# Half-size products for four of eight feature pairs, two banks for the second product, and a listed order of steps

## The chip, the core and the metric

The kernel runs on one core of one Trainium2 chip. The metric is the device time of one execution in microseconds (us). Before the change it is 716.3 us, the median of three executions (715.98 to 716.58).

## The reference

An attention across channels is followed by a two-layer network with a tanh GELU. All inputs and the output are float32.

```python
# q, k, v: (4, 6080, 256); w_in: (256, 2048); w_out: (2048, 256)
qn = q / (norm(q, axis=1) + 1e-6);  kn = k / (norm(k, axis=1) + 1e-6)
s = kn.transpose(0, 2, 1) @ qn / tau            # (4, 256, 256)
a = softmax(s, axis=-1)
x = (v @ a).reshape(24320, 256)
h = x @ w_in                                    # (24320, 2048)
g = 0.5 * h * (1 + tanh(c * (h + 0.044715 * h**3)))
out = g @ w_out                                 # (24320, 256)
```

## The kernel before, in words

For each of the four batches the kernel forms the Gram matrix of q and k (256 x 256) and the column norms, and from them the attention matrix. That matrix is multiplied into `w_in` once per batch (`aw_part`, L422), which leaves one 256 x 2048 matrix `AW`. So h = v @ AW, and the tokens see two matrix products: the first (256 to 2048 features) and, after the GELU, the second (2048 to 256).

**Blocks.** Tokens are taken in blocks of 512, twelve in a batch (the last has 448), 48 in all, numbered n. In the loop at the end of the kernel each block has eight stages, one per pair p of feature chunks (two chunks of 128 features, so 256 features a pair).

**First product.** `mm1` (L442, matmuls at L450) does a pair with four matmuls of 512 columns (two feature chunks, two halves of the 256 input channels), into a pair of banks of PSUM, the memory that TensorE writes to. There are two such pairs of banks (pool `pH`). One ScalarE instruction (L454) applies the GELU to both chunks, 1024 elements a partition, and writes bf16 to `g`.

**Second product.** It runs one block behind. It is already a 2 x 2 Strassen-Winograd product: the features in two halves, the tokens of a block in two halves, seven products instead of eight. Each product (`product`, L531, matmuls at L546) is eight matmuls of 256 columns. Its left factors, sums of parts of `w_out`, are made once. Its right factors are sums of parts of `g`, made per block on VectorE (DVE): t1 at L517 (2048 elements), t2, t3, t4 at L528 to L530 (1024 elements, two calls each). The seven products accumulate in three single banks (`r`, `p`, `q` of pool `pM`): ScalarE copies partial results out (`keep`, L555), DVE adds them to later ones (`add_out`, L562) and transposes the outcome in 32 x 32 squares (`turn`, L570), and four DMAs store it (`store`, L647).

**The next batch, meanwhile.** In blocks 1 to 7 of a batch the rows of q and k of the next one, loaded as bf16 through GpSimd's queue (`load_one`, L93), go through the Gram product, two matmuls of 256 columns per 128 rows (`gram_row`, L213). ScalarE squares q (L165), DVE squares k (L166), and DVE folds the squares into one 128 x 512 float32 tile (`sum_rows`, L188 to L202). In block 8 DVE splits that tile into three bf16 parts (`split`, L242 to L246) whose columns TensorE sums with twelve one-column matmuls (`ss_cols`, L259). Blocks 9 to 11 form the scores, the row sums and `AW` of the next batch.

**Order.** Everything is issued in the order of the program text (`manual_schedule`); every engine runs its own instructions strictly in that order, and the framework adds the waits. The loop calls, in each stage p, `mm1` with its GELU, then one product of the second product, then what that stage has of sums, Gram row, fold and chain.

The kernel's pool `pM` has four tags of one bank each: `a` (Gram, then products into `AW`), `q`, `p`, `r`.

Of the kernel before, what the change touches and what calls it, by code (L numbers as in the profile page):

```python
# [17 lines left out]
def kernel(  # L18
# [38 lines left out]
    tsp = ctx.enter_context(tc.tile_pool(name="tsp", bufs=2))  # L57
# [6 lines left out]

    pM = ctx.enter_context(tc.tile_pool(name="pM", bufs=1, space=bass.MemoryType.PSUM))
    pH = ctx.enter_context(tc.tile_pool(name="pH", bufs=2, space=bass.MemoryType.PSUM))


    def chunks_of(b):
        sizes = [8, 7, 8, 8, 8, 6, 2] if b == 0 else [7, 7, 7, 7, 7, 7, 5]  # L70
        assert sum(sizes) == R
        res, r0 = [], 0
        for n in sizes:
            res.append((r0, n))
            r0 += n
        return res
# [77 lines left out]

    def squares(b, c):
        qt, kt = qk_tiles[b, c]
        r0, n = chunks_of(b)[c]
        rest = with_rest(b, c)
        sq = sqp.tile([128, 8, 512], BF16, tag="sq")
        if rest:  # L160
            nc.vector.memset(sq[REM:, n, :], 0.0)
        if n <= 2:
            nc.vector.tensor_mul(sq[:, 0:n, 0:256], qt[:, 0:n, :], qt[:, 0:n, :])
        else:
            nc.scalar.activation(sq[:, 0:n, 0:256], qt[:, 0:n, :], AF.Square)  # L165
        nc.vector.tensor_mul(sq[:, 0:n, 256:512], kt[:, 0:n, :], kt[:, 0:n, :])  # L166
        if rest:
            nc.scalar.activation(sq[:REM, n, 0:256], qt[:REM, n, :], AF.Square)
            nc.vector.tensor_mul(sq[:REM, n, 256:512], kt[:REM, n, :], kt[:REM, n, :])
        SQ[b, c] = sq  # L170
# [11 lines left out]
    def sum_rows(b, c):  # L182

        sq = SQ.pop((b, c))
        n = len(rows_of(b, c))
        assert n in (6, 7)
        a1 = addp.tile([128, 4, 512], BF16, tag="a1")
        nc.vector.tensor_add(a1[:, 0:3, :], sq[:, 0:3, :], sq[:, 3:6, :])  # L188
        a2 = addp.tile([128, 2, 512], FP32, tag="a2")
        nc.vector.tensor_add(a2[:, 0, :], a1[:, 0, :], a1[:, 1, :])  # L190
        if n == 7:
            nc.vector.tensor_add(a2[:, 1, :], a1[:, 2, :], sq[:, 6, :])
        rest = a2[:, 1, :] if n == 7 else a1[:, 2, :]
        if b not in ACC:
            acc = accp.tile([128, 512], FP32, tag="acc")
            ACC[b] = acc
            nc.vector.tensor_add(acc, a2[:, 0, :], rest)
        else:
            acc = ACC[b]
            a3 = addp.tile([128, 512], FP32, tag="a3")  # L200
            nc.vector.tensor_add(a3, a2[:, 0, :], rest)
            nc.vector.tensor_add(acc, acc, a3)  # L202

    def gram_row(b, c, i):
        if (b, c, i) == (b, 0, 0):
            G[b] = pM.tile([128, 2, 256], FP32, tag="a", name=f"G{b}")
# [3 lines left out]
        first = c == 0 and i == 0  # L210
        last = c == len(chunks_of(b)) - 1 and i == len(rows) - 1
        for jc in range(2):
# [4 lines left out]
                start=first and jc == 0, stop=last and jc == 1)  # L217

    def ss_rows(c, which):
# [3 lines left out]
        if c == 0:  # L223
            SS[which] = pM.tile([128, 2] if which == 0 else [128, 256], FP32,
                                tag="qp"[which], name=f"ss0{which}")
# [14 lines left out]
    def split(parts, rest, x):  # L240

        nc.vector.tensor_copy(parts[0], x)  # L242
        nc.vector.tensor_sub(rest, x, parts[0])
        nc.vector.tensor_copy(parts[1], rest)
        nc.vector.tensor_sub(rest, rest, parts[1])
        nc.vector.tensor_copy(parts[2], rest)  # L246

    def ss_split(b):
        parts = addp.tile([128, 4, 512], BF16, tag="a1", name=f"parts{b}")
        rest = addp.tile([128, 2, 512], FP32, tag="a2", name=f"rest{b}")  # L250
        split([parts[:, i, :] for i in range(3)], rest[:, 0, :], ACC[b])
        ACC[b] = parts

    def ss_cols(b):

        SS[b] = pM.tile([128, 4], FP32, tag="q", name=f"ss{b}")
        for j in range(4):
            for i in range(3):
                nc.tensor.matmul(SS[b][:, j : j + 1], lhsT=ACC[b][:, i, j * 128 : j * 128 + 128],  # L259
                                 rhs=ones_bf[:, 0:1], start=j == 0 and i == 0,  # L260
                                 stop=j == 3 and i == 2)
# [46 lines left out]
    def first_aw():  # L308
# [3 lines left out]
        ps = [pM.tile([128, 512], FP32, tag="qp"[ic], name=f"aw_ps{ic}") for ic in range(2)]  # L312
# [37 lines left out]
    def k_factors(b):  # L350
# [6 lines left out]
        parts = smx.tile([128, 3, 2], BF16, tag="parts")  # L357
        rest = smx.tile([128, 2], FP32, tag="rest")
        split([parts[:, i, :] for i in range(3)], rest, rr[:, 2:4])
        NRM[b] = (parts, rh)  # L360

    def k_row(b):

        parts, rh = NRM[b]
        dg = smx.tile([128, 3, 2, 128], BF16, tag="dg")
        for i in range(3):
            for ic in range(2):
                nc.vector.tensor_mul(dg[:, i, ic, :], ident_bf,
                                     parts[:, i, ic : ic + 1].to_broadcast([128, 128]))
# [91 lines left out]

# [353 lines left out]
```

## Time and profile before

| what | value |
|---|---|
| time, median of 3 | 716.3 us |
| granted TensorE clock | 0.999 of full speed |
| TensorE (PE) busy | 693.9 us, 4885 matmuls |
| VectorE (DVE) busy | 521.5 us, 950 instructions |
| ScalarE (ACT) busy | 485.9 us, 590 instructions |
| first product, L450, 512 columns | 1344 + 64 matmuls (and 128 of 448 columns) |
| second product, L546, 256 columns | 2464 matmuls (and 224 of 224 columns) |
| Gram rows, L213 | 368 matmuls of 256 columns |
| GELU, L454, 1024 elements | 352 instructions, 1024 ns each |
| t2, t3, t4, 1024 elements | 88 each, 0.67 to 0.68 us each |

The profile gives for each engine the time in which at least one of its instructions ran. Matmuls overlap in the pipeline, so a matmul's duration (about 0.38 us for 512 columns) is longer than the slot it takes in the stream; the distance from one start to the next gives the slot. The chain of waits follows the work that ended last back to its start. A timeline row merges equal instructions: start, length, engine, line, operation, count.

### The profile page before, as it was taken

The page shows a single profiled execution, that of the slowest core. Times are in us where ns is not written, and L with a number is a line of the kernel's source. Part 1 is how long each engine was busy: PE and PEld are TensorE (multiplying, and loading weights), DVE is VectorE, ACT ScalarE, POOL GpSimd, SP SyncE. Part 2 cuts the span into 40 slices and gives each one's busy share as a digit, 9 for nine tenths or more (in the row PEclk, how much of TensorE's full clock was granted, in tenths as well). Part 3 has the DMA queues.
Part 4 walks back from the last instruction along what each step waited for, and adds up shares of the span by engine and source line. Part 5 has one row for each costly group of instructions (what it writes and reads, how often), then busy time and mean ns, then how long its engine had stood idle before and what let it go on. Part 6 is the DMA issues. An engine that isn't in the chain of part 4 may idle for free.

```text
span 716.3 us, 12307 instructions
## 1 busy us (share of the span) xinstructions
PE 693.9 (97%) x4885; PEld 467.7 (65%) x4885; DVE 521.5 (73%) x950; ACT 485.9 (68%) x590; POOL 67.1 (9%) x125
## 2 busy tenths in 40 slices
PE   3899999999999999999999999999999999999997
PEld 2756666666666666666666666666666666666665
DVE  4589878778957887878875778788786465564565
ACT  5387667766677677666767676676677666666673
POOL 4320011100001011101001010110000000000000
PEclk9999999999999999999999999999999999999999
DMA  9998778832558888744427787775334336354122
GB/s 241 208 253 149 135 124 143 132 64 58 98 84 132 141 145 131 128 80 94 80 59 140 99 153 132 126 125 102 58 72 99 62 68 103 67 95 81 43 59 56
DMA packets 161402, 79.19 MB, mean 111 GB/s; under 512 B 150368, under 2 KB 153184, under 8 KB 160352
## 3 DMA queue, kind: packets, MB, share of 16 engines
q0 software_dynamic: 12576, 39.46, 34.9%
q1 hardware_dynamic: 147664, 37.67, 25.3%
q10 hardware_dynamic: 1104, 1.28, 0.6%
q8 instruction: 38, 0.62, 0.4%
q14 instruction: 20, 0.16, 0.1%
HBM read 78.91 MB, written 36.83 MB: 162 GB/s over the span
## 4 chain that ended last, share of the span: by engine, by line
PE 90%; DMA 5%; DVE 2%; issue 1%; ACT 0%; POOL 0%; DVEq 0%; POOLq 0%
PE hp L450 44%; PE r L546 23%; PE p L546 11%; PE q L546 5%; PE G L213 5%; DMA t<-in_k_dram 4%; PE ps L426 2%; DMA t<-in_q_dram 1%; DVE sq L166 0%; DVE c L562 0%; DVE ot L570 0%; PE ss L237 0%; DVE t L530 0%; DVE a L177 0%; DVE wcomb L499 0%
## 5 line engine op out<-in xcount | busy, mean ns | idle before, releaser
L454 ACT ACTIVATE g<-hp 128x1024 bf16<-128x1024 f32 (+1 forms) x384 | 386.7, 1015 | 195.8 <-PE hp L450 191.4
L450 PE MATMUL hp<-vT,aw 128*128 128x512 bf16 (+1 forms) x1472 | 370.2, 377 | 0.0
L546 PEld LDWEIGHTS <-wcomb 128*128 128x128 bf16 x2688 | 262.5, 98 | 101.6 <-issue 6.1
L450 PEld LDWEIGHTS <-aw 128*128 128x128 bf16 x1536 | 149.5, 98 | 110.1 <-issue 1.1
L546 PE MATMUL r<-t,wcomb 128*128 128x256 bf16 (+1 forms) x1152 | 148.1, 271 | 1.4 <-DVE c L562 1.1
L562 DVE TENSOR_TENSOR c<-r,y 128x256 f32<-128x256 f32 (+1 forms) x95 | 39.9, 420 | 50.5 <-PE r L546 42.9
L213 PE MATMUL G<-t 128*128 128x256 bf16 (+1 forms) x368 | 64.3, 273 | 3.3 <-DMA t<-in_k_dram 3.3
L530 DVE TENSOR_TENSOR t<-t,g 128x1024 bf16<-128x1024 bf16 (+1 forms) x96 | 65.0, 677 | 0.0
L529 DVE TENSOR_TENSOR t<-g 128x1024 bf16<-128x1024 bf16 (+1 forms) x96 | 64.9, 676 | 0.0
L562 DVE TENSOR_TENSOR c<-q,x 128x256 f32<-128x256 f32 (+1 forms) x48 | 20.1, 419 | 60.9 <-PE q L546 56.6
L528 DVE TENSOR_TENSOR t<-g,t 128x1024 bf16<-128x1024 bf16 (+1 forms) x96 | 63.3, 659 | 0.4
L570 DVE STREAM_TRANSPOSE ot<-c 128x256 f32<-128x256 f32 (+1 forms) x144 | 57.6, 425 | 1.9 <-DVE c L562 0.2
L132 POOL DMA_DIRECT2D vb<-in_v_dram x46 | 23.6, 512 | 376.8 <-PE hp L450 376.8
L517 DVE TENSOR_TENSOR t<-g 128x2048 bf16<-128x2048 bf16 (+1 forms) x48 | 57.7, 1203 | 0.0
L165 ACT ACTIVATE sq<-t 128x1792 bf16<-128x1792 bf16 (+3 forms) x26 | 43.1, 1657 | 9.8 <-DMA t<-in_q_dram 9.8
L546 PE MATMUL q<-g,wcomb 128*128 128x256 bf16 (+1 forms) x384 | 49.3, 271 | 0.0
L546 PE MATMUL p<-t,wcomb 128*128 128x256 bf16 (+1 forms) x384 | 49.3, 271 | 0.0
L546 PE MATMUL p<-g,wcomb 128*128 128x256 bf16 (+1 forms) x384 | 49.3, 271 | 0.0
L546 PE MATMUL r<-g,wcomb 128*128 128x256 bf16 (+1 forms) x384 | 49.3, 271 | 0.0
L213 PEld LDWEIGHTS <-t 128*128 128x128 bf16 (+1 forms) x368 | 35.6, 98 | 12.5 <-issue 4.6
L570 DVE STREAM_TRANSPOSE ot<-r 128x256 f32<-128x256 f32 (+1 forms) x48 | 21.4, 445 | 30.6 <-PE r L546 30.6
L166 DVE TENSOR_TENSOR sq<-t 128x1792 bf16<-128x1792 bf16 (+4 forms) x27 | 28.1, 1042 | 11.7 <-DMA t<-in_k_dram 11.4
(110 smaller groups left out, 344.3 us busy)
## 6 DMA issues: line engine op xcount, KB each, us to landing
out_dram<-ot SPq DMA_DIRECT2D x176, 128.0 KB, 2.4
vb<-in_v_dram POOLq DMA_DIRECT2D x42, 256.0 KB, 4.7
t<-in_q_dram POOLq DMA_DIRECT2D x19, 448.0 KB, 5.2
t<-in_k_dram POOLq DMA_DIRECT2D x19, 448.0 KB, 4.9
wst<-in_moe_w_out_dram POOLq DMA_DIRECT2D x2, 1024.0 KB, 10.2
t<-in_q_dram POOLq DMA_DIRECT2D x3, 512.0 KB, 15.0
t<-in_k_dram POOLq DMA_DIRECT2D x3, 512.0 KB, 16.9
out_dram<-ot SPq DMA_DIRECT2D x12, 112.0 KB, 4.9
```

Source lines behind the costliest of these rows:

```text
L165: nc.scalar.activation(sq[:, 0:n, 0:256], qt[:, 0:n, :], AF.Square)
L166: nc.vector.tensor_mul(sq[:, 0:n, 256:512], kt[:, 0:n, :], kt[:, 0:n, :])
L213: nc.tensor.matmul(G[b][:, jc, :], lhsT=qt[:np_, r, jc * 128 : jc * 128 + 128], rhs=kt[:np_, r, :], start=first and jc == 0, stop=last and ...
L450: mm = nc.tensor.matmul(hp[:, u, :cols], lhsT=AW[b][:, cc, fc * 128 : fc * 128 + 128], rhs=vt_tiles[n][:, cc, :cols], start=cc == 0, stop= ...
L454: nc.scalar.activation(GS[n][:, 2 * p : 2 * p + 2, :cols], hp[:, :, :cols], AF.Gelu_apprx_tanh)
L517: nc.vector.tensor_sub(t1[:, :, :hc], quarter(n, 0, 1), quarter(n, 0, 0))
L528: nc.vector.tensor_sub(v[2], b22, v[1])
L529: nc.vector.tensor_sub(v[3], b22, quarter(n, 0, 1, f0, f1))
L530: nc.vector.tensor_sub(v[4], v[2], quarter(n, 1, 0, f0, f1))
L546: nc.tensor.matmul(ACCS[n, acc][:, :hc], lhsT=wcomb[:, w, fc, :], rhs=x, start=first and fc == 0, stop=fc == 7, skip_group_check=True)
L562: nc.vector.tensor_add(CS[n][:, tj, ci, :hc], ACCS[n, acc][:, :hc], XS[n, name][:, :hc])
L570: nc.vector.transpose(OT[n][:, tj * nb : tj * nb + nb, ci, :], src.rearrange("p (x t) -> p x t", t=32))
```

## The change

**Half-size products in the first product (`small`, `set_step`, `sums_w`, `sums_v`).** Two pairs of feature chunks form a set; the sets are pairs (1, 2) and (5, 6). A set is a 2 x 2 product: feature pair by half of the input channels, times half of the input channels by half of the tokens. In place of 2 pairs x 4 matmuls of 512 columns it does seven products m1 to m7, two matmuls of 256 columns each. The left factors are parts of `AW` and four sums of them (`sums_w`, eight DVE operations a batch); the right factors are parts of v and four differences (`sums_v`, three DVE operations a block). A set uses one pair of banks `qp` and one single bank `rb` (tag `s`). Its steps, for set i, by their names in the lists:

- `m1` into rb; `cq`: ScalarE copies rb to the first half of qp, where `m2` will be added; `m5` into the second half of qp; `y5`: ScalarE copies that to SBUF (`yw`).
- `m6` is added to rb; `ap`: DVE writes rb + yw to the second half of qp, where `m3` will be added.
- `m7` is added to rb; `ax`: DVE writes rb + yw to SBUF (`xw`); `m4` is added to rb.
- GELUs: `Gq` from qp (1024 elements), `Gr` from rb (512), `Gx` from xw (512).

Blocks 0 and 1 and blocks 10 and 11 of batches 0 to 2 have no set and block 2 has one; all others have two.

**Second product in two banks.** It now uses `r` and `p` only (in blocks without sets `s` also, for one product). The fifth product stays in `p` after being copied; DVE writes r + copy back to `p` (`ap`), where the third product is added; `p` is then transposed straight from PSUM. A product is issued in two halves (`M1A`, `M1B`), the sums in halves (`T2a`, `T2b`, ...).

**A listed order.** A block's steps follow one of three lists, GRAM, PLAIN and NO_SETS. A name ending in -1 means that step for the block before, -2 two before, +1 one ahead; g0 is the first product of pair 0, G0 its GELU, w0m1 step m1 of set 0, M1A the first half of product 1, c11 to c22 and c11a the second product's adds and transposes, e0 to e7 the places for loads and for the chain to the next batch. Where the list changes from one block to the next, steps that the new one has with a shorter lag are issued first.

**The Gram stage.** Eight chunks of six rows (the last five and a rest) in blocks 1 to 8 in place of seven; both squares on ScalarE; the fold in single steps f1 to f5. The splits into three bf16 parts go: the column sums take four one-column float32 matmuls and the row of k factors one float32 matmul of 256 columns. ScalarE copies the Gram matrix to SBUF, and the chain to the next batch moves to blocks 9 to 11.

The core of the diff:

```diff
-    tsp = ctx.enter_context(tc.tile_pool(name="tsp", bufs=2))
+    tsp = ctx.enter_context(tc.tile_pool(name="tsp", bufs=1))
+    t4p = ctx.enter_context(tc.tile_pool(name="t4p", bufs=2))
...
-    pH = ctx.enter_context(tc.tile_pool(name="pH", bufs=2, space=bass.MemoryType.PSUM))
+    pH = ctx.enter_context(tc.tile_pool(name="pH", bufs=1, space=bass.MemoryType.PSUM))
...
-        sizes = [8, 7, 8, 8, 8, 6, 2] if b == 0 else [7, 7, 7, 7, 7, 7, 5]
+        sizes = [8, 7, 8, 8, 8, 6, 2] if b == 0 else [6, 6, 6, 6, 6, 6, 6, 5]
...
-            for i in range(3):
-                nc.tensor.matmul(SS[b][:, j : j + 1], lhsT=ACC[b][:, i, j * 128 : j * 128 + 128],
-                                 rhs=ones_bf[:, 0:1], start=j == 0 and i == 0,
-                                 stop=j == 3 and i == 2)
+            nc.tensor.matmul(SS[b][:, j : j + 1], lhsT=ACC[b][:, j * 128 : j * 128 + 128],
+                             rhs=ones_f[:, 0:1], start=True, stop=True)
...
-        for i in range(3):
-            nc.tensor.matmul(ps, lhsT=ones_bf, rhs=dg[:, i], start=i == 0, stop=i == 2)
+        nc.tensor.matmul(ps, lhsT=ones_f, rhs=dg, start=True, stop=True)
...
+    def small(n, i, m):
...
+        lhs, rhs = {1: (aw(pa, 0), v[:, 0, lo]), 2: (aw(pa, 1), v[:, 1, lo]),
+                    3: (sw(4), v[:, 1, hi]), 4: (aw(pb, 1), tv[:, 3, :hc]),
+                    5: (sw(1), tv[:, 0, :hc]), 6: (sw(2), tv[:, 2, :hc]),
+                    7: (sw(3), tv[:, 1, :hc])}[m]
+        if m == 1:
+            RB[n, i] = pM.tile([128, 512], FP32, tag="s", name=f"rb{n}_{i}")
+        dst = {2: 0, 3: 1, 5: 1}
+        acc = qp(n, i)[:, dst[m]] if m in dst else RB[n, i]
...
+        for u in range(2):
+            nc.tensor.matmul(acc[:, u * hc : u * hc + hc], lhsT=lhs[:, u * 128 : u * 128 + 128],
+                             rhs=rhs, start=m in (1, 5) and u == 0, stop=u == 1,
+                             skip_group_check=True)
...
+    def set_step(n, i, what):
...
+        if what == "cq":
+            nc.scalar.activation(qp(n, i)[:, 0, :c], RB[n, i][:, :c], AF.Copy)
+        if what == "y5":
+            YW[n, i] = xp.tile([128, 512], FP32, tag="yw", name=f"yw{n}_{i}")
+            nc.scalar.activation(YW[n, i][:, :c], qp(n, i)[:, 1, :c], AF.Copy)
+        if what == "ap":
+            nc.vector.tensor_add(qp(n, i)[:, 1, :c], RB[n, i][:, :c], YW[n, i][:, :c])
+        if what == "ax":
+            XW[n, i] = xp.tile([128, 512], FP32, tag="xw", name=f"xw{n}_{i}")
+            nc.vector.tensor_add(XW[n, i][:, :c], RB[n, i][:, :c], YW.pop((n, i))[:, :c])
...
+    GRAM = steps(
+        "g0 c21-2 w1Gr-1 e0 c11-3 w0m5 G0 row3 T2a-1 M1A-1 w0m1 T2b-1 M1B-1 w0cq c11a-2 g3 "
+        "e1 w0y5 T3b-1 cq-1 w0m6 row1 G3 w0ap M5A-1 M5B-1 e2 T3a-1 qsq w0m7 M6A-1 w0ax row5 "
+        "M6B-1 c22-2 y5-1 w0m4 T4b-1 e3 w0m3 w0Gr w0m2 w1m5 ap-1 row0 w0Gq f3-1 row2 w1m1 "
+        "M3A-1 vs+1 e4 w1cq M3B-1 w1y5 row4 T4a-1 w1m6 g4 w0Gx w1ap e5 M7A-1 c12-1 G4 w1m7 "
+        "T1a w1m3 w1m2 M7B-1 ksq M2A-1 w1ax e6 g7 ax-1 w1Gx f1 M4B-1 w1Gq w1m4 e7 M4A-1 "
+        "f4-1 M2B-1 G7 f2")
+    PLAIN = steps(
+        "g0 c11a-2 w1Gr-1 c22-2 e0 M1A-1 G0 T3b-1 w0m1 w0m5 M1B-1 T2b-1 w0cq M5A-1 e1 T2a-1 "
+        "w0y5 w0m6 M5B-1 w0ap g3 y5-1 T4b-1 cq-1 e2 w0m7 G3 M6A-1 w0ax M6B-1 w0m3 e3 ap-1 "
+        "w0m4 w1m5 T3a-1 w0Gr w0m2 M3A-1 w0Gq M3B-1 w1m1 e4 c12-1 M7A-1 w1cq vs+1 g4 w0Gx "
+        "w1y5 T4a-1 w1m6 e5 M7B-1 G4 w1ap M2A-1 M2B-1 ax-1 w1m2 c11-2 e6 w1m3 w1m7 w1Gq "
+        "M4A-1 w1ax g7 T1a w1Gx e7 M4B-1 G7 w1m4 c21-1")
...
+            if (blk, p) == (9, 2):
+                for k in range(1, 6):
+                    todo((f"f{k}", n - 1))
...
+        CHAIN = {
+            (9, 0): [g_copy],
+            (9, 3): [ss_cols, norms],
+            (9, 5): [k_factors, k_row],
+            (9, 7): [k_row_pe],
+            (10, 0): [scores_b, lambda b: scores_c(b, 0)],
...
+            (11, 0): [row_sums],
+        }
```

## The prediction

> **What bounds the kernel now.** I read the page's busy times first, then the stages, then single instructions. Busy share by engine, and the chain of waits:
>
> ```profile
> PE 693.9 (97%) x4885; PEld 467.7 (65%) x4885; DVE 521.5 (73%) x950; ACT 485.9 (68%) x590; POOL 67.1 (9%) x125
> ...
> PE 90%; DMA 5%; DVE 2%; issue 1%; ACT 0%; POOL 0%; DVEq 0%; POOLq 0%
> ```
>
> TensorE (PE) is busy for 97% and carries 90% of the chain; the rest is mostly the loading at the start. A busy share is only an average, so I asked for busy times over single blocks (columns: length; busy time and count of PE, weight loads, DVE, ACT, POOL; clock; DMA share; GB/s): a block with Gram rows, the one after it, one of the last batch.
>
> ```profile
> 294.90:309.40 14.50, 14.48 (x103) 9.75 (x101) 11.75 (x21) 10.26 (x12) 2.65 (x5) 1.00 0.76 123
> ...
> 323.90:337.00 13.10, 13.10 (x100) 8.81 (x99) 10.07 (x27) 8.71 (x12) 1.53 (x2) 1.00 0.37 70
> ...
> 573.00:586.00 13.00, 13.00 (x89) 8.61 (x88) 7.54 (x15) 8.93 (x11) 0.49 (x1) 1.00 0.47 83
> ```
>
> TensorE never pauses in any of them. So the time is the sum of matmul slots, and nothing but fewer slots (or new pauses) moves it. The slot comes from starts, not durations, since matmuls overlap. Timeline of one block:
>
> ```profile
> 326.53 1.03 PE L450 MATMUL hp<-vT,aw 128*128 128x512 bf16 x4
> ...
> 327.40 1.04 PE L546 MATMUL q<-g,wcomb 128*128 128x256 bf16 x8
> ...
> 328.27 1.03 PE L450 MATMUL hp<-vT,aw 128*128 128x512 bf16 x4
> ```
>
> Four 512-column matmuls take 0.87 us, eight 256-column ones 0.87: 0.2175 and 0.109 us each, exactly by columns. A plain block is 32 x 0.2175 + 56 x 0.109 = 13.0 us; 14 Gram matmuls add 1.5, as the windows show.
>
> The other engines must be priced by spacing too. DVE back to back:
>
> ```profile
> 324.32 0.69 DVE L528 TENSOR_TENSOR t<-g,t 128x1024 bf16<-128x1024 bf16 x1
> ...
> 324.93 0.69 DVE L529 TENSOR_TENSOR t<-g 128x1024 bf16<-128x1024 bf16 x1
> ...
> 325.53 0.68 DVE L530 TENSOR_TENSOR t<-t,g 128x1024 bf16<-128x1024 bf16 x1
> ```
>
> A sum of 0.68 to 0.69 us costs 0.60 in a full queue: 0.08 overlaps. And two group rows for prices:
>
> ```profile
> L454 ACT ACTIVATE g<-hp 128x1024 bf16<-128x1024 f32 x352 | 357.8, 1024 | 183.6 <-PE hp L450 179.8 <-DVE aw L433 1.8
> ...
> L562 DVE TENSOR_TENSOR c<-q,x 128x256 f32<-128x256 f32 x44 | 18.6, 423 | 53.5 <-PE q L546 49.2 <-ACT g L454 4.3
> ```
>
> [...] the trace has 1024 ns for 1024 elements [...] and two gelus in 1.94 us from 323.26, so 0.92 apart. [...] the trace has 692 ns at 512 and 423 from PSUM at 256, [...] no fp32 matmul is in this trace.
>
> **The change, part by part.**
>
> *Half-size products.* Listed by block: n=0, 1 and the six blocks 10 and 11 of batches 0 to 2 have no set, n=2 has one, the other 39 two: 79 sets. A set replaces 8 matmuls of 512 columns (1.74 us) by 14 of 256 (1.526): 0.217 saved. 77 x 0.217 + 2 x 0.19 (last block, 448 columns) = **-17.1 us**. There are six more weight loads per set, at 98 ns each below the 109 ns slot, so they stay under the matmuls as L546's do.
>
> *What the sets put elsewhere.* Per set ACT gets two 512-element copies (the first product, PSUM to PSUM; the fifth, to SBUF) and three gelus (1024, 512, 512) for two of 1024. Unseen forms; by the 256-element keep (385 ns) and the 1024-element gelu a 512 one is 0.60 us, spaced 0.50. DVE gets two 512-element fp32 adds (0.69, spaced 0.61); per block 0.98 us of token differences. A plain block with two sets then needs, in spacings, ACT 4 x 0.92 + 2 x (0.92 + 4 x 0.50) + 2 x 0.27 = 10.1 us, and DVE 12.0 us by durations (0.98 + 4 x 0.69 + 1.21 + 6 x 0.68 + 7 x 0.43), 10.5 by spacings, against 12.57 on TensorE. A Gram block (12 Gram matmuls now) is 13.88 on TensorE; both squares on ACT make 10.1 + 2 x 1.37 = 12.8; the fold on DVE (0.91 + 3 x 0.69) makes 15.0 by durations, but 25 x 0.08 overlaps: 13.0. So each engine is left some per cent, DVE least.
>
> *Whether the order fits.* I walked the lists, each PE step at its slot, releases 0.2 us after a slot's end (hp started 301.39, slot to 302.26, gelu at 302.45). Plain block, times from its start: w0m1 ends 1.52, but ACT has the previous set's last gelu until 0.95 and G0 at 1.07 to 1.98, so w0cq runs 1.98 to 2.58; w0m6 is due at 2.60. y5 ends 3.07; DVE does c21, c11a, c22, T3b, T2b, T2a until 3.1, then w0ap to 3.8; w0m7 is due at 4.12. w0ax 4.54 to 5.23, w0m4 due 5.42. Second set: cq ends 7.96 (due 8.46), ap 9.7 (10.41), ax 11.5 (12.37). Banks: w1m5 at 5.64 needs G3's end 5.34; c21 is out at 0.5, the first second-product at 0.87. Behind a late w0cq would stand y5, G3 and the rest of ACT; behind a late w0ap all DVE sums, for which the second product waits. Gram block: w0ap ends 4.36 (due 4.55), w0ax 5.68 (5.85), w1m6's copy 8.27 (8.46), w1ap 9.6 (9.98); DVE's fold waits for the k squares at 12.1 and ends 0.4 into the next block, where c21 is needed only at 1.30. Slack is 0.02 to 0.5 us everywhere, nothing is late. I take 0.05 us lost per block with sets, **+2 us** (0 to 0.25, so 0 to 10).
>
> *Loads.* The k load is issued behind g4's matmuls (9.5 in the block), and row3 uses it 5.4 us later, where it had 7:
>
> ```profile
> t<-in_k_dram POOLq DMA_DIRECT2D x19, 448.0 KB, 4.9
> ...
> t<-in_k_dram POOLq DMA_DIRECT2D x3, 320.0 KB, 4.2
> ```
>
> 384 KB between these: 4.55 us plus 0.2, so 0.6 spare. Free.
>
> *The chain to the next batch.* Out of PE go 36 one-column matmuls (0.30 us per 12 by starts), 9 of 256 columns (1.0 us) and 12 one-column row sums (0.4): -2.3. In come 12 one-column fp32 and three 256-column fp32 matmuls; [...]: +2.9. Net **+0.5** (-1.5 to +4). In block 9 two folds (0.69 each) are queued ahead of w0ax, which then ends at 6.4 where w0m4 is due at 5.42, and the column sums wait for them: 1.0 us, three times, **+3** (0 to 6). DVE's five-op splits that go relieve a queue that did not bind.
>
> *Second product in two banks, steps in a list.* Same 56 matmuls, same keeps less one (ACT 0.27 us), an add and turns as before: no PE slot changes. Costed at nothing, TensorE's stream being the cover. At the twelve switches between lists leftover steps are flushed at once ahead of the new list: 0.1 each, **+1.2**. At the end one more set's gelu stands before the last sums: **+0.5**.
>
> Sum: 716.3 - 17.1 + 2 + 0.5 + 3 + 1.2 + 0.5 = 706.4, say **706.5 us**.
>
> **Rivals.** *All of it is kept* (no pauses; matmul slots alone): 716.3 - 17.1 + 0.5 and the tail's 0.5 give 700. For it: my walk found no late step in a steady block. Against: block 9. *DVE becomes the bound in Gram blocks*: if it does not overlap, 15.0 against 13.88 us over 23 such blocks adds 25 us: 730, slower than before. For it: 15.0 is the sum of durations; against: before's Gram block held 13.0 us of durations (sums 5.3, outputs 3.0, k squares 1.1, fold 3.7) in 11.75 us of busy time. *The ladder is slower than its rungs*: each set passes its single bank PE-ACT-PE-DVE-PE-DVE-PE-ACT in a fixed order. Were a copy or add with PSUM on both sides 0.25 us dearer than my rows, w0cq alone would stop TensorE 0.25 us and its followers some more, 0.4 a block: 39 x 0.4 on top of the forecast is 720, slower. For it: 0.02 us of slack there; against: nothing in the rows makes a PSUM target dearer.
>
> **Numbers.** The forecast's case (701.5 to 713) 0.60, all kept (below 701.5) 0.15, a ladder or DVE that eats most of the gain (713 to 714.9) 0.06, all of it within 0.2% 0.04, slower through DVE or the ladder 0.15. Faster is thus 0.81. The range from 699.5 (no pause, chain terms low) to 717 leaves some 0.03 below and 0.15 above.
>
> **What would show it.** Right: plain blocks of 12.6 us and Gram blocks of 13.9, TensorE without idle in them, DVE 85 to 95% busy, and about a microsecond of idle on TensorE in block 9 ahead of w0m4. Wrong: TensorE idle before the small products behind ScalarE or VectorE (the ladder), DVE over 97% in Gram blocks, rows waiting for the k load, or small products spaced over 0.11 us.

## Result: the time does not change, and the profile after

The changed kernel takes 717.2 us (717.09 to 717.33), the kernel before 716.4 us beside it; the ratio is 1.0012, 95% interval 0.9995 to 1.003. No difference can be measured. The forecast was 706.5 us, so it was wrong, by 10.7 us.

Busy times and chain of waits of the profile after:

```profile
PE 682.2 (95%) x5335; PEld 515.5 (72%) x5335; DVE 610.5 (85%) x1174; ACT 595.3 (83%) x828; POOL 69.8 (10%) x131
...
PE 79%; DVE 11%; DMA 6%; issue 2%; ACT 1%; POOL 0%; DVEq 0%; POOLq 0%; ACTq 0%
```

TensorE has 11.7 us less to do (693.9 before), and the span is only 1.0 us shorter (715.3 for 716.3). The rest is idle time, and the chain now runs through VectorE for 11% where it was 2%. The average does not tell where, so again single blocks: one with Gram rows, blocks 9, 10 and 11 of a batch, one of the last batch (columns as before: length; busy time and count of PE, weight loads, DVE, ACT, POOL; clock; DMA share; GB/s).

```profile
307.50:321.40 13.90, 13.90 (x114) 10.94 (x112) 13.23 (x26) 13.34 (x19) 2.65 (x5) 1.00 0.80 128
...
335.70:351.10 15.40, 14.29 (x113) 10.92 (x111) 12.80 (x28) 12.27 (x20) 1.53 (x2) 1.00 0.51 83
351.10:364.50 13.40, 13.16 (x90) 8.59 (x88) 12.07 (x23) 9.92 (x15) 0.55 (x1) 1.00 0.56 101
364.50:381.40 16.90, 16.14 (x109) 10.33 (x108) 13.42 (x30) 11.32 (x16) 0.49 (x1) 1.00 0.40 64
589.00:601.60 12.60, 12.60 (x102) 9.72 (x101) 10.81 (x22) 10.82 (x17) 0.49 (x1) 1.00 0.50 85
```

The first and the last line are the steady stages, and they are as forecast: 13.9 and 12.6 us, no idle on TensorE, VectorE 95% and 86% busy. The three between are not: TensorE stands still for 1.1 us in block 9, 0.2 in block 10 and 0.8 in block 11.

The rows of the new operations, from the groups by line:

```profile
L505 ACT ACTIVATE g<-h 128x1024 bf16<-128x1024 f32 (+1 forms) x226 | 227.6, 1011 | 43.6 <-PE h L495 41.0 <-DVE aw L435 1.8
...
L579 DVE TENSOR_TENSOR qp<-rb,yw 128x512 f32<-128x512 f32 (+1 forms) x79 | 54.9, 695 | 24.9 <-ACT x L725 16.1 <-ACT yw L577 8.7
...
L577 ACT ACTIVATE yw<-qp 128x512 f32<-128x512 f32 (+1 forms) x79 | 46.9, 594 | 2.0
L574 ACT ACTIVATE qp<-rb 128x512 f32<-128x512 f32 (+1 forms) x79 | 46.4, 588 | 5.5 <-PE rb L564 2.4
...
L731 DVE TENSOR_TENSOR c<-r,y 128x256 f32<-128x256 f32 (+1 forms) x48 | 19.6, 408 | 2.5 <-PE r L716 2.5
```

The copies were put at 0.60 us and the adds at 0.69; they take 0.59 and 0.70, and the copy with PSUM on both sides (L574) no more than the one to SBUF (L577). These prices were not the fault.

To find the fault I took the distance from the first matmul of each block to that of the next, and subtracted the slots of its matmuls (0.1085 us for 256 columns, by columns, and 0.025 for one column). What is left I call lost; it holds waits, and what float32 matmuls take above these slots. In us:

| blocks | lost before | lost after |
|---|---|---|
| 1 and 2 | 1.5 | 4.7 |
| the 19 full blocks with Gram rows: 3 to 7, 13 to 19, 25 to 31 | 5.4 | 2.3 |
| 8, 20, 32 | 0.0 | 1.1 |
| 9, 21, 33 | 0.0 | 7.3 |
| 10, 22, 34 | 0.0 | 1.2 |
| 11, 23, 35 | 0.6 | 3.5 |
| 12, 24, 36 | 0.1 | 0.8 |
| 37 to 46 | 0.1 | 0.6 |
| 47, the last | 0.2 | 1.5 |
| block 0 | 0.4 | 0.4 |
| **sum** | **8.3** | **23.5** |

The slots themselves fell from 664.3 to 646.4 us, 17.9 less. Of that 15.2 comes back as lost time, 2.0 after the last block (7.05 us for 5.0), and the start is 0.3 earlier: -17.9 + 15.2 + 2.0 - 0.3 = -1.0, the difference of the spans. The gain is all there, and it is given back at the edges of the batches, above all in blocks 8 to 12, 13.2 us more than before over three passes.

The two spans differ by -1.0, the medians by +0.8, because the profiled execution of the kernel before took 718.07 us, 1.7 above the median of 716.4. As much stands in its block 25 (16.3 us, where its other full Gram blocks take 14.5 to 14.7), in one wait for rows of k:

```profile
PE G L213 <- DMA t<-in_k_dram: 3.3, 3, 1.6
```

The longest of these three waits (1.6 us) is the one in block 25. If it is what sets this execution apart, a usual one of the kernel before loses about 6.6 us and not 8.3, and the change puts nearer 17 than 15 us of loss in place of its 17.9 us of slots.

**Block 9.** Timeline of block 21 (columns: start, length, engine, line, operation, count; in brackets the idle time before it and what ended it):

```profile
336.79 0.65 DVE L219 TENSOR_TENSOR f<-f,a 128x512 f32<-128x512 f32 x1
...
337.47 0.69 DVE L219 TENSOR_TENSOR acc<-f,acc 128x512 f32<-128x512 f32 x1
...
338.08 0.42 DVE L731 TENSOR_TENSOR c<-p,x 128x256 f32<-128x256 f32 x1
...
338.55 0.60 PE L716 MATMUL p<-t,wcomb 128*128 128x256 bf16 x4 [0.49 <-DVE c L731]
...
340.54 0.69 DVE L579 TENSOR_TENSOR qp<-rb,yw 128x512 f32<-128x512 f32 x1
...
341.29 0.38 PE L564 MATMUL rb<-tv,sw 128*128 128x256 bf16 x2 [0.62 <-DVE qp L579]
...
342.60 0.95 PE L262 MATMUL ss<-ones_f,acc 128*128 128x1 f32 x8
...
343.41 0.38 PE L564 MATMUL rb<-tv,aw 128*128 128x256 bf16 x2
```

The two folds at L219 stand at the head of the block. They are `f3` and `f4` of the Gram block before; the list PLAIN has no such step, so they are issued at the switch, ahead of the new list. Behind them wait c11a (L731), for which M5A stands, and at the end of the same queue w0ap (L579), for which w0m7 stands. Against the slots these two waits are 0.65 and 0.79 us. Then the column sums: four float32 one-column matmuls, recorded as two each, take 0.95 us (0.81 of the stream, from their first start at 342.60 to that of the next product at 343.41); in the kernel before twelve bf16 ones took 0.30, counted the same way.

**Block 11.** Timeline of block 23:

```profile
366.25 0.24 PE L414 MATMUL sums<-ones_bf,eT 128*128 128x1 bf16 x4
...
366.42 0.68 DVE L693 TENSOR_TENSOR t<-t,g 128x1024 bf16<-128x1024 bf16 x1
...
367.02 0.17 DVE L418 RECIPROCAL rs<-sums 128x2 f32<-128x2 f32 x1
367.24 0.59 PE L428 MATMUL ps<-win_bf,eT 128*128 128x512 bf16 x2 [0.74 <-DVE rs L418]
```

The row sums lie in bank `a`, and the first product into AW (L428) needs the same bank. So TensorE waits until VectorE has read them, and VectorE has a sum t in hand. In the kernel before the row sums lay in bank `q`, which the change took away.

**Blocks 1 and 2.** Timeline of block 2:

```profile
68.21 0.69 DVE L219 TENSOR_TENSOR acc<-f,a 128x512 f32<-128x512 f32 x1
68.82 0.69 DVE L689 TENSOR_TENSOR t<-g,t 128x1024 bf16<-128x1024 bf16 x1
69.42 0.69 DVE L691 TENSOR_TENSOR t<-g 128x1024 bf16<-128x1024 bf16 x1
70.02 0.69 DVE L579 TENSOR_TENSOR qp<-rb,yw 128x512 f32<-128x512 f32 x1
```

and TensorE in the same stretch:

```profile
68.22 1.04 PE L716 MATMUL p<-t,wcomb 128*128 128x256 bf16 x8
70.77 0.38 PE L564 MATMUL rb<-tv,sw 128*128 128x256 bf16 x2 [1.51 <-DVE qp L579]
...
74.06 1.02 PE L495 MATMUL h<-vT,aw 128*128 128x512 bf16 x4 [0.73 <-ACT g L584]
```

Again w0ap (L579) comes late on VectorE, here behind the whole fold of the first chunk, and TensorE stands 1.5 us. In block 1, which has no set, it stands 1.7 us for an add of the second product, which VectorE does after squaring k (for this first chunk still VectorE's work); in the kernel before it stood 1.1 there. (The starts 68.82, 69.42, 70.02 also show the 0.60 us spacing that the forecast took.)

### The profile page after: what moved, and what is told of

Its sections match the earlier page's. It is cut to its first block, busy times and chain, and to the rows that moved or that the text cites. A ratio compares the mean times of both kernels' runs of the same rounds, so it can differ in the third digit from the quotient of the medians.

```text
span 715.3 us, 13755 instructions
## 1 busy us (share of the span) xinstructions
PE 682.2 (95%) x5335; PEld 515.5 (72%) x5335; DVE 610.5 (85%) x1174; ACT 595.3 (83%) x828; POOL 69.8 (10%) x131
## 4 chain that ended last, share of the span: by engine, by line
PE 79%; DVE 11%; DMA 6%; issue 2%; ACT 1%; POOL 0%; DVEq 0%; POOLq 0%; ACTq 0%
PE h L495 22%; PE r L716 20%; PE p L716 15%; PE rb L564 9%; PE qp L564 7%; PE G L230 4%; DMA t<-in_k_dram 3%; DMA wst<-in_moe_w_out_dram 2%; PE ps L428 2%; DVE ot L740 1%; DMA t<-in_q_dram 1%; DVE t L677 1%; DVE t L693 1%; DVE t L689 1%; DVE t L691 1%
## 5 line engine op out<-in xcount | busy, mean ns | idle before, releaser
L505 ACT ACTIVATE g<-h 128x1024 bf16<-128x1024 f32 (+1 forms) x226 | 227.6, 1011 | 43.6 <-PE h L495 41.0
L495 PE MATMUL h<-vT,aw 128*128 128x512 bf16 (+1 forms) x840 | 212.1, 375 | 0.7 <-ACT g L584 0.7
L495 PEld LDWEIGHTS <-aw 128*128 128x128 bf16 x904 | 88.4, 98 | 65.6 <-issue 1.6
L584 ACT ACTIVATE g<-qp 128x1024 bf16<-128x1024 f32 (+1 forms) x79 | 80.2, 1015 | 9.5 <-PE qp L564 9.2
L176 ACT ACTIVATE sq<-t 128x1536 bf16<-128x1536 bf16 (+4 forms) x59 | 79.5, 1361 | 9.6 <-DMA t<-in_q_dram 9.6
L564 PEld LDWEIGHTS <-sw 128*128 128x128 bf16 x632 | 61.5, 98 | 29.0 <-issue 5.3
L579 DVE TENSOR_TENSOR qp<-rb,yw 128x512 f32<-128x512 f32 (+1 forms) x79 | 54.9, 695 | 24.9 <-ACT x L725 16.1
L564 PE MATMUL rb<-tv,sw 128*128 128x256 bf16 (+1 forms) x316 | 60.1, 272 | 3.6 <-DVE qp L579 3.4
L582 DVE TENSOR_TENSOR xw<-rb,yw 128x512 f32<-128x512 f32 (+1 forms) x79 | 54.3, 687 | 8.7 <-PE rb L564 8.1
L589 ACT ACTIVATE g<-rb 128x512 bf16<-128x512 f32 (+1 forms) x79 | 47.1, 597 | 16.4 <-PE rb L564 13.9
L136 POOL DMA_DIRECT2D vb<-in_v_dram x46 | 23.1, 502 | 356.6 <-PE h L495 356.6
L574 ACT ACTIVATE qp<-rb 128x512 f32<-128x512 f32 (+1 forms) x79 | 46.4, 588 | 5.5 <-PE rb L564 2.4
```

The costliest lines, as they stand in the source:

```text
L176: nc.scalar.activation(o, t[:np_, r, :], AF.Square)
L495: mm = nc.tensor.matmul(hp[:, u, :cols], lhsT=AW[b][:, cc, fc * 128 : fc * 128 + 128], rhs=vt_tiles[n][:, cc, :cols], start=cc == 0, stop= ...
L505: nc.scalar.activation(gs(n)[:, 2 * p : 2 * p + 2, :cols], HP.pop((n, p))[:, :, :cols], AF.Gelu_apprx_tanh)
L564: nc.tensor.matmul(acc[:, u * hc : u * hc + hc], lhsT=lhs[:, u * 128 : u * 128 + 128], rhs=rhs, start=m in (1, 5) and u == 0, stop=u == 1, ...
L579: nc.vector.tensor_add(qp(n, i)[:, 1, :c], RB[n, i][:, :c], YW[n, i][:, :c])
L584: nc.scalar.activation(gs(n)[:, 2 * pa : 2 * pa + 2, :c].rearrange("p u (t x) -> p t u x", t=2), QP.pop((n, i))[:, :, :c].rearrange("p t ( ...
```

## Experiments

All ratios are to the kernel before, run beside each kernel on the same chip, with the 95% interval. The changed kernel was timed in four executions only, and not beside these kernels, so a difference between a median here and its 717.2 us is uncertain by a microsecond or more. The block lengths of the profiles are steadier: those of blocks 9 to 12 that an edit does not touch agree within 0.02 us. "Lost" is as above.

### Row sums in another bank

```diff
-        ps = pM.tile([128, 2], FP32, tag="a", name=f"sums{b}")
+        ps = pM.tile([128, 2], FP32, tag="s", name=f"sums{b}")
```

> The changed kernel with one edit: the row sums of the next batch's attention (block 11) go to bank s in place of bank a, which the first product into AW also uses. Theory 'edges' (the half-size products keep their gain, and it is given back at the batch edges): in block 11 TensorE waits 0.88 us for the reciprocal of the row sums to have read bank a before it may write AW's first product there; three batches, so 2.6 us less than the changed kernel's 717.2: 714.6. Rival 'the wait only moves': the eviction of AW needs the reciprocal anyway, so the time stays within 0.5 us of 717.2.

Measured: 716.01 us, ratio 0.9987 (0.998 to 0.9994). Block 11 falls from 16.89 to 16.00 us in all three batches, so 0.89 us a batch is the shared bank's. The sum, 2.7 us, is not in the median: in this profile the Gram blocks lost 4.2 us in place of 2.3, to k loads that came late (1.3 us in block 25). That spread is taken up below.

### The last blocks' adds first

```diff
+        for key in (("c11a", 46), ("w1Gr", 47), ("c22", 46), ("T2b", 47), ("T2a", 47), ("c11", 46)):
+            todo(key)
         for what, lag in order_of(NN - 1):
```

> The changed kernel with one edit: at the end, the last adds and transposes of block 46 and the sums t2 of block 47 are issued before t3 and t4 of block 47. Theory 'edges': the sixth product waits 0.7 us for t2 because t3 is queued ahead of it, and the stores of block 46 leave at 706 only, so that block 47's wait in the same queue until 710.9 although DVE is done at 709.0; together 2.5 us less: 714.7. Rival 'transfers end when they end': the end is set by the last store of block 47 alone; at most 0.7 us less: 716.5.

Measured: 717.49 us, ratio 1.0013 (1.0001 to 1.0024). From the start of block 47 to the end it is 24.6 us, for 25.5, so the order costs 0.9 us there; it does not show in the median. Of the 2.9 us that the end is longer than before, most stays. One part of it can be read in the profile after: block 46's stores are issued late, and block 47's last stores stand behind them.

```profile
705.87 0.44 DVE L740 STREAM_TRANSPOSE ot<-c 128x256 f32<-128x256 f32 x1
...
706.34 4.41 SPq L831 DMA_DIRECT2D out_dram<-ot  x4
...
708.64 0.38 DVE L740 STREAM_TRANSPOSE ot<-r 128x224 f32<-128x224 f32 x1
...
710.85 1.95 SPq L820 DMA_DIRECT2D out_dram<-ot  x4
```

The four stores of block 46 (L831) hold their queue for 4.4 us, from a transpose at 705.87, and the last stores of block 47 (L820) stand behind them 1.8 us after the last transpose has ended (709.02). Why the fourth store of block 46 waits until a store of block 47 has landed was not settled.

### The two folds of block 9 later

```diff
-            if (blk, p) == (9, 2):
-                for k in range(1, 6):
-                    todo((f"f{k}", n - 1))
+            if (blk, p) in ((9, 4), (9, 5)):
+                todo((f"f{p - 1}", n - 1))
...
-            (9, 3): [ss_cols, norms],
-            (9, 5): [k_factors, k_row],
-            (9, 7): [k_row_pe],
-            (10, 0): [scores_b, lambda b: scores_c(b, 0)],
+            (9, 6): [ss_cols, norms],
+            (10, 0): [k_factors, k_row],
+            (10, 1): [k_row_pe],
+            (10, 2): [scores_b, lambda b: scores_c(b, 0)],
...
-                    if lag > max(lags.get(what, 0), what in SECOND) and what[0] != "e":
+                    if lag > max(lags.get(what, 0), what in SECOND) and what[0] not in "ef":
```

(The score steps of block 10 are drawn together accordingly.)

> The changed kernel with one edit: the last two fold steps of a batch's squares are no longer issued at the start of block 9 but at its places 4 and 5, behind the first set's adds; the column sums go to place 6 and the steps behind them up to three places later. Theory 'edges': the two folds (0.61 us each on DVE) stand ahead of c11a and of the first set's ap, and TensorE waits 0.65 us for the one and 0.79 us for the other; these 1.44 us go in three batches, some 0.2 us each come back in blocks 9 and 10: 4 us less than 717.2, so 713.2. Rival 'ladder': the set's chain itself is late in block 9, the folds only happen to stand there, and as much is lost behind ap and ax: within 1 us of 717.2.

Measured: 717.81 us, ratio 1.0017 (1.001 to 1.0025). Block 9 falls from 15.44 to 13.88 us, so the folds at its head did cause the waits there. Block 10 rises from 13.43 to 14.81. From the timeline of TensorE in this run, the second pass through block 10:

```profile
353.95 0.70 PE L378 MATMUL rk<-dg,ones_f 128*128 128x256 f32 x2 [0.63 <-ACT dg L371]
```

The row of k factors (L378), now in block 10, waits for ScalarE, which waits for VectorE's reciprocal. The chain from fold to scores is long, and a step that is moved back takes its wait along. Of the 1.56 us gained a batch, 1.38 come back (0.22 of each are the row's own slots, which went from the one block to the other).

### The last batch without half-size products

```diff
-        return 0 if n // NB < B - 1 and blk in (10, 11) else 2
+        return 0 if n // NB == B - 1 or blk in (10, 11) else 2
```

> The changed kernel with the half-size products taken out of the last batch alone (blocks 36 to 47 use eight full products and the list without sets; all else is kept). Theory 'edges': the ten steady blocks 37 to 46 go from 12.64 to about 13.05 us, 4.1 us, block 36 by 0.3, and in the end 1 us is won back since no set stands at the end: 717.2 + 3.5 = 720.7. Rival 'the sets bring nothing in a steady block' (their small products and waits cost what they save): 717.2 or less.

Measured: 719.37 us, ratio 1.0032 (1.0011 to 1.0052). A plain block goes from 12.64 to 13.02 us. A steady one, to be held against the last line of the windows above:

```profile
593.00:606.00 13.00, 13.00 (x91) 8.59 (x88) 7.54 (x16) 8.94 (x11) 0.49 (x1) 1.00 0.61 84
```

Ten blocks at 0.38 us are 3.8 us; block 36 is 0.14 longer, block 47 is 0.87 shorter (17.58, as before), and the end of the span 22.8 us after block 47's start in place of 25.5. So 3.9 - 2.6 = 1.3 us are expected from the blocks against the span of the changed kernel, and 2.2 were measured in the median (2.0 in the spans: this run's row waits and start add another 0.6). The half-size products gain in steady blocks what their slots say, but for 0.05 us a block.

### Both loads earlier

```diff
-            if p in (2, 5) and blk < len(chunks_of(nxt)):
-                load_one(nxt, blk, p // 5, gate)
+            if p in (1, 3) and blk < len(chunks_of(nxt)):
+                load_one(nxt, blk, p // 3, gate)
```

> The changed kernel with one edit: the loads of the next q and k chunks stand at places 1 and 3 of a block in place of 2 and 5, so k is issued some 6 us earlier. Theory 'k lands at its deadline': in the changed kernel k lands 0.6 to 1.3 us into the next block, where TensorE wants it at about 1.1; the Gram blocks that lose 0.1 to 1.4 us at random (0.7 us in the first trace, 3 us in that of the run with the row sums in bank s) all come back to 13.93, and the executions spread less: about 1 us less than 717.2, so 716.2. Rival 'the transfers only collide elsewhere': the earlier load meets the transposes and the stores at the block's start, lands later itself or delays v, and the time stays or rises.

Measured: 730.19 us (722.17 to 730.46), ratio 1.0148 (1.0104 to 1.0192): 13 us slower in the median. In its profile the loss is in two blocks, 13 and 25, which take the first chunk of the third and of the fourth batch: 20.7 and 21.8 us, where the changed kernel has 14.5 and 14.0. The other full Gram blocks take 13.93, but for one with 14.2, so there the early loads did remove the waits. TensorE in block 13:

```profile
228.05 0.59 PE L230 MATMUL G<-t 128*128 128x256 bf16 x2 [4.21 <-DMA t<-in_k_dram]
...
230.56 1.91 PE L495 MATMUL h<-vT,aw 128*128 128x512 bf16 x4
```

It stands for rows of k until 228.05, and in block 25 for another 5.7 us until 406.2. Each of the two cost more than itself. For 4.9 us after the first one, four matmuls of 512 columns that took 1.03 us take 1.91. In that window the granted clock (the third number from the end) is 0.50:

```profile
228.10:232.60 4.50, 4.50 (x18) 2.59 (x18) 0.00 (x0) 1.54 (x4) 0.00 (x0) 0.50 0.35 73
```

The stops are 4.4 and 5.9 us by the slots, and the slow stretches after them add 2.4 and 2.1. The page of this run shows a lower clock (8 tenths for 9) in the two of its 40 slices that hold these stops, and else only in the last.

DMA issues of the stretch from 205 to 240 us, in which the first stop falls (median us to landing at the end):

```profile
t<-in_k_dram POOLq DMA_DIRECT2D x2, 384.0 KB, 9.2
...
vT<-vb SPq DMA_TRANSPOSE x3, 10.6
```

and of the same stretch of the changed kernel:

```profile
t<-in_k_dram POOLq DMA_DIRECT2D x2, 384.0 KB, 4.7
...
vT<-vb SPq DMA_TRANSPOSE x3, 5.6
```

The q load is issued at 212.3, 0.5 us after the load of v and 0.2 after v's transposes, and the k load at 215.3. The four are in flight together and all take longer: the k load 12.7 us, landing at 228.0, the q load 13.6. In the changed kernel the q load follows v's by 3.5 us and the k load comes another 4.1 later. The loads of GpSimd's queue and the transposes of the other are stretched alike: by the medians above, 9.2 us for 4.7 (k) and 10.6 for 5.6. So an earlier load was not by itself a load that lands earlier (228.0 here, 224.6 in the changed kernel), and two blocks in which it lands late outweigh all others.

### Block 9 without half-size products

```diff
-        return 0 if n // NB < B - 1 and blk in (10, 11) else 2
+        return 0 if n // NB < B - 1 and blk in (9, 10, 11) else 2
```

This kernel leaves out the last transpose and the store of block 7 of batches 0 to 2: the step c11 of two blocks back belongs to neither list at this switch.

> The changed kernel with one edit: block 9 of batches 0 to 2 takes full products and the list without sets, as blocks 10 and 11 do. Theory 'DVE queue': the folds and the chain to the next batch then have room on DVE, nothing on TensorE waits for a set's add, and block 9 goes from 15.44 to about 14.2 us although three blocks lose their 0.43 us of saving: 3 x 1.2 less than 717.2, so 713.6. Rival 'the chain is what costs' (float32 column sums, TensorE's wait for the fold): block 9 stays at 15.4 or more and the time at 717.2 or above.

Measured: 714.21 us, ratio 0.9968 (0.9958 to 0.9979). The same edit with that step put back:

```diff
+                if order is NO_SETS:
+                    todo(("c11", n - 2))
```

> Block 9 of batches 0 to 2 without half-size products, alone, and with the last transpose and store of block 7 put back that the earlier kernel of this kind left out. If the 3 us that the earlier kernel gained come from the ladder of block 9, it gives 714.5 us (713.5 to 715.5). If they came from the work left out, it gives 717.

Measured: 714.53 us, ratio 0.9971 (0.9959 to 0.9983), so the work left out was not the gain. The window of block 9, to be held against 15.40 us above:

```profile
335.90:350.30 14.40, 14.40 (x101) 9.78 (x99) 11.98 (x28) 10.44 (x16) 1.53 (x2) 1.00 0.67 108
```

1.03 us less in each of three batches, though its slots are 0.43 more. Without sets nothing on TensorE hangs on the place of w0ap in VectorE's queue, and this block's waits for VectorE are gone. What stays lost (0.98) is mostly the float32 column sums, which take 0.81 us of the stream in the changed kernel.

### The start

```diff
-                    squares(nxt, 0)
+                    square(nxt, 0, 0, "act")
+                if p == 6:
+                    square(nxt, 0, 1, "act")
...
-                if p == 7:
-                    for k in range(1, 6):
-                        todo((f"f{k}", 1))
+            if (n, p) == (2, 4):
+                for k in range(1, 6):
+                    todo((f"f{k}", 1))
```

> The changed kernel with two edits in batch 0: the fold of the first chunk moves from the end of block 1 to place 4 of block 2, and the first chunk's k is squared on ScalarE at place 6 of block 1 in place of DVE at place 4. Theory 'DVE queue': in block 2 TensorE waits 1.67 us for the first set's ap, behind which four sums and three folds stand, and then 0.89 for a bank; in block 1 it waits 1.7 us for an add queued behind the square. Block 2 goes from 16.69 to about 14.3 and block 1 from 16.2 to 15.4: 3 us less than 717.2, so 714.2. Rival 'start-up': the waits come from the weights' preparation and the first transfers; at most 0.7 us less.

Measured: 714.96 us, ratio 0.9973 (0.9965 to 0.9982), 2.2 us under the changed kernel. Block 2 falls from 16.69 to 15.02 us: the fold's place in VectorE's queue was the 1.67 us wait there. Block 1 falls by 0.7 (0.4 against its length in other runs without this edit), of which k's square, moved to ScalarE from ahead of the late add, is the likely cause. The wait for the bank of `h` (0.7 idle in the timeline above, 0.9 against the slots) stays.

### All of it together

First with the early loads in it, and with the store of block 7 of batches 0 to 2 left out as above:

> The changed kernel with all of these edits: row sums in bank s, early loads, block 9 with full products, the two edits of the start, the third reciprocal of the scores one place earlier in block 10, and at the end the sums t2 and t3 of block 47 and the adds of block 46 ahead of t4. Theory 'edges': the gains add up, 2.6 + 1 + 3.6 + 3 + 1 + 1.5 = 12.7 us less than 717.2: 704.5. Rival 'one wait replaces the other': each edit moves its wait to the next consumer, as the moved folds did in block 10; 712 or more.

Measured: 726.06 us, ratio 1.0117 (1.0083 to 1.0151). Blocks 2, 13 and 25 take 22.0, 21.5 and 23.1 us: the early loads cover everything else. Then without them, and whole: the row sums' bank, the start, block 9 without sets (with c11), the last but one of the score steps of block 10 (its third reciprocal) one place earlier, (10, 4) for (10, 5), and the last blocks' adds first, now with T3b and T3a in that list too.

> Five edits of the changed kernel together, the whole of the reference's output computed: row sums in bank s, the start's squares and fold moved, block 9 of batches 0 to 2 without half-size products, the last score step one place earlier, the last blocks' adds ahead of the last sums. If the losses at the edges of a batch are separate and each edit removes its own, the time is 717.2 - 2.6 (row sums) - 2.3 (start) - 3.0 (block 9) - 0.7 (score step, end) = 708.6 us, between 706 and 711, below the kernel before. If each edit only moves its wait to the next one in the chain, it stays above 714.

Measured: 707.48 us, ratio 0.9867 (0.9854 to 0.9881). And with the k load one place earlier on top:

```diff
-            if p in (2, 5) and blk < len(chunks_of(nxt)):
-                load_one(nxt, blk, p // 5, gate)
+            if p in (2, 4) and blk < len(chunks_of(nxt)):
+                load_one(nxt, blk, p // 4, gate)
```

> The combined kernel with the k load one place earlier in its block (place 4 of 8 in place of 5, some 1.7 us sooner), the q load unchanged at place 2. If the k rows arrive with no slack and nothing else is in flight in that stretch, the waits before the k rows go and the time falls by 1 to 3 us against the combined kernel. If the earlier k load overlaps the q load and the v loads, as with both loads early, it takes longer and the time stays or rises by 2 us and more.

Measured: 705.40 us (705.21 to 705.56), ratio 0.9840 (0.9826 to 0.9853). This is 11 us below the kernel before and 12 below the changed one. Its chain, and its windows of a Gram block and of blocks 9, 10 and 11:

```profile
PE 91%; DMA 4%; DVE 3%; ACT 0%; issue 0%; POOL 0%; DVEq 0%; POOLq 0%
```

```profile
301.60:315.50 13.90, 13.90 (x114) 10.93 (x112) 13.23 (x26) 13.34 (x19) 2.65 (x5) 1.00 0.88 129
...
329.80:344.20 14.40, 14.40 (x101) 9.78 (x99) 11.99 (x28) 10.44 (x16) 1.53 (x2) 1.00 0.63 108
344.20:357.20 13.00, 13.00 (x90) 8.58 (x89) 10.98 (x19) 9.95 (x14) 0.55 (x1) 1.00 0.52 81
357.20:373.10 15.90, 15.88 (x110) 10.27 (x109) 13.22 (x30) 11.33 (x16) 0.49 (x1) 1.00 0.39 70
```

VectorE is out of the chain again (3%), and TensorE idle in none of the four but for 0.02 us. By blocks, the span falls from 715.3 to 703.4: blocks 1 and 2 give 2.6, block 9 of three batches 3.1, block 10 1.2 (the score step), block 11 3.0, the Gram blocks 1.2 (the k load), block 47 and what follows 0.9. These sum to 12.0, rounded, for 11.9. Each edit removed its own wait, and no wait took its place.

GpSimd's queue in that Gram block shows what the k load's one place did. Changed kernel, block 19, then the combined one, same block:

```profile
311.45 0.55 POOL L97 DMA_DIRECT2D t<-in_q_dram  x1 [2.13 <-ACT x L725]
...
317.77 0.55 POOL L97 DMA_DIRECT2D t<-in_k_dram  x1 [5.24 <-ACT g L592]
```

```profile
305.55 0.55 POOL L97 DMA_DIRECT2D t<-in_q_dram  x1 [2.13 <-ACT x L725]
...
306.62 0.55 POOL L97 DMA_DIRECT2D t<-in_k_dram  x1
```

The view names a GELU of ScalarE (L592), but that one had ended at 316.94, 0.8 us before the load. The queue was held by the code: `extras` holds each load until the matmuls of the first product that were issued last before it have ended, and at place 5 those are g4's:

```profile
316.21 1.03 PE L495 MATMUL h<-vT,aw 128*128 128x512 bf16 x4
```

These end at 317.24, and the load starts at 317.77. One place earlier the load is tied to g3's matmuls, which have long ended, so it starts over 5 us sooner in its block, not 1.7 as I had expected. It takes longer (8.5 us in the median beside the q load, for 4.6 in the combined kernel with the load at its old place), and still lands ahead of its rows: all 19 full Gram blocks take 13.93 us. With the k load at its old place, they lost between 1.2 and 3.3 us more than their floor in the profiles of four of the kernels that share that stage (changed kernel 1.2, row sums 3.1, block 9 whole 3.3, combined 2.4; the floor is 19 x 0.06 = 1.1). A spread of 2 us is as large as what a single edit gains.

## Why the prediction was wrong

**What held.** The half-size products' -17.1 us: the slots fell by 17.9 in all, 0.8 of it the matmuls that the chain to the next batch no longer has, and the kernel without sets in its last batch shows 0.38 us a block, where two sets should save 0.43 and 0.06 is lost. The steady walk: plain blocks 12.64 us, Gram blocks 13.93, forecast 12.6 and 13.9. The term of +2 for a loss in each of those blocks was the right size (0.06 for 0.05), and the change even removed 0.15 us a Gram block: the kernel before lost 0.2 in each of them, which "TensorE never pauses" overlooked. Two rivals fall with this. VectorE does not become the bound in Gram blocks: it is busy 13.23 of 13.90 us, and TensorE does not wait. The ladder is no slower than its rungs where the lists are steady.

**What failed.** The forecast's sum had +7.2 us for all that is not slots (2 + 0.5 + 3 + 1.2 + 0.5). Measured it is +17.2 (15.2 between the matmuls of the blocks, 2.0 at the end), or some 18.9 without the wait in block 25 of the kernel before. By its steps:

- *Block 9, +3.* The mechanism was right, VectorE's folds ahead of a step of the ladder, but the place was wrong. I had the folds ahead of w0ax, at place 2 of the block; the switch issues them ahead of the block's whole list, so M5A stands for c11a and w0m7 for w0ap: 1.44 us a batch, 4.3 in all.
- *Small and float32 matmuls, net +0.5.* Both prices were estimates of mine that no trace supported, since the kernel before has no float32 matmul. The one-column ones were put at 0.13 us each and take 0.20 of the stream (0.81 for four). That is 0.9 us more over three batches. The row of 256 columns was put at 0.44 and was right: two recorded matmuls, 0.43 us together, as much as four bf16 slots of 0.109. For one column that measure does not hold: four bf16 slots of 0.025 would be 0.1.
- *Second product in two banks, "costed at nothing".* This step failed by its reasoning and not only by its size. I asked only whether the second product had fewer slots, not who else had lived in bank `q`. The row sums had; moved to bank `a` they put a VectorE instruction between two matmuls: 0.88 us a batch, 2.6 in all.
- *Twelve switches of list, +1.2.* Block 9's apart, what is left is block 12 with 0.8 us, so the term was not too small. Block 10's 1.2 us are no switch but the third reciprocal of the score steps, as its move by one place shows (0.42 to 0.01 in each batch), and had no term. Block 8's 1.1 us are small gaps around the rows of the last, partial chunk, which stood in block 7 before.
- *The start, in no term.* I walked steady blocks only. In block 2 the first set meets the fold of a chunk on VectorE, 2.3 us more lost than before; in block 1 an add of the second product comes late there, 0.9 more. That is 3.2 us.
- *The end, +0.5.* It is 2.9 us from the start of block 47 on; 0.9 of it was the order of the last adds.
- *Loads, "0.6 spare. Free".* There was none to spare: in block 19 the k load starts 10.3 us into the block (317.77), where 9.5 was taken, and TensorE waits for k rows in some blocks, 0.6 us at most in this profile and 1.3 in others. In sum that is 0.9 us here, and the kernel before had such waits too (1.7 us in block 25 of its profile).

The forecast's change was -9.9 us, the medians' +0.8, a gap of 10.7. The table accounts for 10.5 of it, the wait in block 25 of the kernel before left out. Block 9 and the chain's matmuls are 3.0 over their terms (7.3 of lost time less 0.8 of slots, for 3.5), block 11 2.9, blocks 1 and 2 3.2, the end 2.8 (3.3 for 0.5), block 10 1.2 and block 8 1.1; that is 14.2. The other way go the steady blocks (2.9, since the term of +2 stood against a loss that fell by 0.9), the switch at block 12 (0.5) and the start (0.3).

The errors at the edges all have one sign, because I walked only the steady blocks queue by queue, and gave what comes at the edges a token price or none. The case that came true, steady stages as forecast and the edges taking all of it, was not among my rivals. The combined kernel, at 705.4 us, shows how much of the gain is left once the edges are mended: it is 5 us above the rival *all of it is kept*. That it lies 1 us below the forecast is chance, since it has other edges, other loads and no sets in block 9. The edits were not tried on the kernel before, which loses time at the start and to k loads too, so it is not shown that all of the 11 us come from the half-size products.

## What to carry to other kernels

When a change takes work off the engine that bounds and puts it on engines in fixed order, cost the edges as carefully as the steady stage: write down each queue at every place where the list of steps changes, at the first block, and at the last. When it takes a memory bank away, list every tile that had used it. And before moving a load earlier, look what else is in flight there, and what the code ties its start to: the k load one place earlier gained 2 us, both loads at places 1 and 3 cost 13, all of it in two blocks.

## What the runs showed that I had not expected

- A one-column float32 matmul cost 0.20 us of the stream here (0.81 for four), eight times a bf16 one (0.025, twelve in 0.30). The profile has two matmuls for each (0.95 us for the eight records), and their weight loads took 192 ns each where those of the bf16 column sums before took 96.
- After TensorE had stood still for 4.4 and 5.9 us (both loads early), its granted clock was 0.50 and a 256-column slot 0.213 us in place of 0.109, for 4.9 and 4.2 us. A stop of 4.4 us cost 6.8.
- Transfers in flight together took longer: the 384 KB load of k took 4.6 us in the median of the changed kernel, 8.5 in that of the kernel which issues it beside the load of q, and 12.7 once, with both loads early, beside the loads of q and v and v's transposes; the median transpose of that stretch took 10.6 for 5.6.
- The 512-element copies and adds that write to PSUM (588 and 695 ns) took what those that write to SBUF took (594 and 687), so a PSUM target was not dearer for these forms.
